# One kernel for attention and two expert layers: head pairs on 64-row scores, one issue order from a list scheduler, 36 weight chunks by way of DRAM

## The chip, the cores and the metric

The kernel runs on 1 core of a Trainium2 chip. The metric is device time in microseconds (us), the median of several executions. Engines that run beside each other: TensorE (PE; the load of its stationary operand is listed as PEld), VectorE (DVE), ScalarE (ACT), GpSimd (POOL), and SyncE (SP), which here only issues DMAs.

## The reference

Everything is float32 at the interface; the weights arrive as float64 and are turned into float32 on the chip.

- Attention: batch 4, 8 heads, 576 tokens, head size 64. `scores = q k^T / 8`, with `min(c_j - c_i, 0)` added, where c is the running sum of `max(s, 0)` along the sequence; causal mask; softmax; times v. That gives x with 2304 rows (tokens) and 512 columns.
- First expert layer: `h = max(x w1, x w2, x w3)` (512 to 768), then `x2 = h w_out` (768 to 512).
- Second expert layer: `h = x2 w_in` (512 to 2048), `g = P(h) / (Q(h) + 1e-6)`, where P is a cubic and Q a quadratic in |h|, then `out = g w_out2` (2048 to 512).

## The kernel before, in words

A float32 product is run as three passes in a format that keeps 12 significant bits: each operand is split into a rounded part hi and the rest lo, and the product is hi hi + hi lo + lo hi (`mm3`, L66). Splitting costs a cast on ACT and a subtraction on DVE or POOL. The value product and the transposes of the attention are plain float32.

**Attention, one head after the other (32 heads).** `load_qk` brings k and q of four heads in one DMA each; `prep_qk` (L177) turns them round with DVE transposes in 32x32 blocks and splits them. The result lies as 32 rows per head with two halves of the head size side by side, so `stage` (L197) copies each head's operands by five more DMAs, from SBUF to SBUF, into tiles `A1`, `B1` and `AB2` with up to 128 rows: the first score matmul contracts 128 rows (hi and lo against hi), the second 68 rows (hi against lo, and four rows that carry the bias). Query rows come in five tiles (64 rows and four times 128), the score blocks in four PSUM banks (`SB`): six blocks, so 12 score matmuls per head (`sc_bank`, L219; the lines L226 and L227). For each block DVE adds the mask and takes the row minimum (L234), ACT takes the exponential with its row sum (L238); `norm` forms the reciprocal on DVE (L244, L245) and POOL scales (L250). `t_bank` transposes the probabilities P on PE (L269, 15 matmuls a head) and copies them out into `PT` (L254 on DVE, L256 on ACT). `pv_pair` (L282) multiplies by v for two heads, each head in its own half of the array's columns (L293), and splits x.

**First expert layer beside it.** `moe1_group` (names m and hs) is 12 matmuls of 288 columns; 144 such groups, 36 for each batch of 8 heads. DVE and ACT take the maximum out of PSUM (L349, L351). A batch's groups can start when the x of its four head pairs is there; they are put between the attention's steps at 4.5 groups a head (`rate`, `credit`, `fill`).

**Weights.** Chunks of 128 x 512 float64 values (512 KB) are loaded and decoded: three bit operations on DVE (L315 to L317), the cast on ACT (L318), the subtraction on POOL (L319). 18 chunks of the first layer (w13) and 18 of the second (`spill`) go through during the attention; the 18 are written to DRAM as hi and lo (512 KB) and read back later. The other 20 (`direct`) are loaded and decoded after the attention's last step, beside the last batch's groups.

**Second half.** For six blocks of 384 tokens: `moe1_out` (mo), then 16 steps of `m2_in` (hp), the rational function on ACT, POOL and DVE (`m2_mid`), and `m2_out` (acc) four steps behind.

**What sets the order.** Tiles are taken from pools; a scheduler of the framework orders the instructions of each engine by a simulated timeline when the program is built. Each engine then runs its queue in order, and waits on semaphores.

Of the kernel before, what the change touches and what calls it, by code (L numbers as in the profile page):

```python
# [14 lines left out]
DRAM = bass.MemoryType.DRAM  # L15


@with_exitstack
def kernel(
# [34 lines left out]
    # query row tiles (first row, rows); columns seen by a tile end at its last row  # L54
# [3 lines left out]
    # the first heads take turns on three sets of score operands, the others on two  # L58
    NF = H

    dma = nc.sync
# [13 lines left out]
    ps_mm = ctx.enter_context(tc.tile_pool(name="ps_mm", bufs=2, space=PSUM))  # L75
# [10 lines left out]
    # weights of the layer at work, 18 chunks of 512 columns in two parts  # L86
# [3 lines left out]
    ps_at = open_pool("ps_at", space=PSUM)  # L90
# [3 lines left out]

    h_dram = dram.tile([DF1, NT], F32, name="h_dram")
    ext_dram = dram.tile([N, 4, 2, S], F32, name="ext_dram")

# [4 lines left out]
    A1 = [at.tile([128, S], F32R, name=f"A1_{i}") for i in range(2)]  # L102
    B1 = [at.tile([128, S], F32R, name=f"B1_{i}") for i in range(2)]
    AB2 = [at.tile([68, 2, S], F32R, name=f"AB2_{i}") for i in range(2)]
    P = [[at.tile([n, 128 * (i + 1)], F32, name=f"P{y}_{i}") for i, (_, n) in enumerate(IT)] for y in range(2)]
    # transposed probabilities of a head pair: row i of column block j at SKEW j + i
# [3 lines left out]
    smalls = [at.tile([128, 4, NI], F32, name=f"small{i}") for i in range(3)]  # L110
    for t in smalls:
        nc.gpsimd.memset(t, 1.0)

    sc = p1.tile([N, 2, S], F32, tag="x", bufs=8, name="sc")
    hl = {}

    def load_qk(g, eng=dma):
        """four heads' k and q rows, 18 tokens a partition, into the place of the hi parts"""
        for nm, src, c in (("k", k, 2), ("q", q, 3)):
            t = at.tile([128, c, 2, S], F32, tag=f"hl{nm}", name=f"hl_{nm}{g}")  # L120
            eng.dma_start(
                out=t[:, 0].rearrange("p c t -> p (c t)"),
                in_=src[g // 2, 4 * (g % 2):4 * (g % 2) + 4].rearrange("h (p f) d -> (h p) (f d)", p=32))
            hl[nm, g] = t

    v_t = {}
    ve_t = {}

    def load_v(pr):
        """v rows of a head pair, the last 64 tokens of two pairs at once"""  # L130
        b, h = divmod(2 * pr, H)
        for n in (2 * pr, 2 * pr + 1):
            v_t[n] = at.tile([128, 4, D], F32, tag="v", bufs=4, name=f"v{n}")
            dma.dma_start(out=v_t[n], in_=v[b, n % H, 0:512].rearrange("(j p) d -> p j d", p=128))
        if pr % 2 == 0:
            ve_t[pr // 2] = at.tile([64, 4, D], F32, tag="ve", bufs=2, name=f"ve{pr // 2}")
            dma.dma_start(out=ve_t[pr // 2], in_=v[b, h:h + 4, 512:576].rearrange("h p d -> p h d"))

    dma.dma_start(out=sc[:, 0, :], in_=s.rearrange("b h s -> (b h) s"))
    load_qk(0)  # L140

    ext = [p1.tile([N, 2, S], F32, tag="x", bufs=8, name=f"ext{r}") for r in range(4)]
    third = [p1.tile([128, 2, S], F32R, tag="x", bufs=8, name=f"third{r}") for r in range(2)]
    A1.append(third[0][:, 0])
    B1.append(third[0][:, 1])
    AB2.append(third[1][0:68])

    def ab_of(n):
        return n % 3 if n < NF else n % 2

    for r in range(4):
        nc.gpsimd.memset(ext[r][:, 1 - r // 2, :], 1.0)
    make_identity(nc, ident)
    nc.gpsimd.memset(mask, 0.0)
    nc.gpsimd.affine_select(
        out=mask[:, S - 128:S], in_=mask[:, S - 128:S], compare_op=ALU.is_ge,
        fill=-BIG / scale, base=0, pattern=[[-1, 128]], channel_multiplier=1)
    for y in range(2):
        for i, t in enumerate(P[y]):
            nc.gpsimd.memset(t[:, 128 * (i + 1) - 64:128 * (i + 1)], 0.0)  # L160
# [3 lines left out]
    c = sc[:, 1, :]  # L164
    nc.vector.tensor_scalar(sc[:, 0, :], sc[:, 0, :], 0.0, 1.0 / scale, ALU.max, ALU.mult)
# [249 lines left out]
    for n in range(3):  # L415
        stage(n)
# [232 lines left out]
```

## Time and profile before

| | us |
|---|---|
| median of 3 runs | 989.79 (988.73 to 990.48) |
| span of the profiled execution, first to last instruction | 991.3 |
| PE busy | 923.2 (93%) |
| DVE busy | 694.2 (70%) |
| ACT busy | 507.9 (51%) |
| POOL busy | 407.5 (41%) |

The profiled execution is one run more; its span is 1.5 us above the median. Busy time of PE is a union of matmuls that overlap in the pipeline, so matmul costs are better read from one start to the next. [...] "Idle before" of a group is the time for which its engine stood still ahead of it.

### The profile page before, as it was taken

Reading aid. Unit: us, or ns where it says so; the run is one execution under the profiler, and the core shown is the slowest. Engines: PE = TensorE matmul, PEld = TensorE weight load, DVE = VectorE, ACT = ScalarE, POOL = GpSimd, SP = SyncE. Lnnn points to the kernel's source line nnn. Section 1 sums busy time; section 2 is a strip of 40 time slices with the busy share of each in tenths; the row PEclk is TensorE's granted clock in tenths of the full one; section 3 lists DMA queues with packets and bytes.
Section 4 is the critical chain, followed back from the end, with each engine's and each line's share of the span. In section 5 each row is a group of like instructions: output and inputs, shape, how many; then the busy total and the mean of one; then the engine's idle time right before and its main releaser. Section 6 shows DMA issues by size and latency. Waiting matters only on the chain.

```text
span 991.3 us, 16031 instructions
## 1 busy us (share of the span) xinstructions
PE 923.2 (93%) x5488; PEld 827.2 (83%) x5488; DVE 694.2 (70%) x1580; ACT 507.9 (51%) x1137; POOL 407.5 (41%) x463
## 2 busy tenths in 40 slices
PE   1688998999989899999979999999999999999997
PEld 1556797888788788999979999999999999999996
DVE  4657787666566574429966886984985885886786
ACT  3656555544444354413235655654664663764664
POOL 2445554435443352203434533542442452452453
PEclk9897999899999899999989999999999999999999
DMA  8886687677787876018883002002000100200000
GB/s 193 195 211 124 178 209 187 162 225 180 211 248 209 230 183 153 20 53 268 277 274 129 1 1 80 1 1 80 1 1 31 50 1 1 80 1 1 33 1 32
DMA packets 77569, 111.87 MB, mean 113 GB/s; under 512 B 24976, under 2 KB 53136, under 8 KB 77488
## 3 DMA queue, kind: packets, MB, share of 16 engines
q1 hardware_dynamic: 77488, 110.86, 40.3%
q8 instruction: 43, 0.70, 0.3%
q14 instruction: 38, 0.31, 0.1%
HBM read 60.70 MB, written 21.82 MB: 83 GB/s over the span
## 4 chain that ended last, share of the span: by engine, by line
PE 65%; DMA 13%; DVE 11%; issue 4%; ACT 3%; POOL 3%; SPq 1%; POOLq 0%; DVEq 0%; ACTq 0%
PE hp L71 18%; PE acc L584 17%; PE m L71 12%; PE mo L71 7%; PE pv L293 5%; PE tr L269 4%; DMA AB<-hl_k 2%; DVE P L234 2%; PE sc L226 1%; PE sc L227 1%; DMA raw<-in_moe_w_in_dram 1%; POOL q L553 1%; POOL q L554 1%; DMA hl_k<-in_k_dram 1%; DVE hs L351 1%
## 5 line engine op out<-in xcount | busy, mean ns | idle before, releaser
L71 PE MATMUL m<-x,w 128*128 128x288 f32 x1728 | 260.1, 305 | 14.5 <-DVE hs L351 14.4
L71 PEld LDWEIGHTS m<-x,w 128*128 128x128 f32 x1728 | 240.8, 194 | 24.8 <-DVE hs L351 19.2
L584 PE MATMUL acc<-ws,g 128*128 128x512 f32 x864 | 217.6, 394 | 1.5 <-ACT g L570 1.5
L553 POOL TENSOR_SCALAR q<-a,cf 128x384 f32<-128x384 f32 x96 | 92.7, 965 | 264.4 <-ACT a L551 249.3
L71 PE MATMUL hp<-x,w2i 128*128 128x384 f32 x1008 | 189.8, 337 | 0.0
L584 PEld LDWEIGHTS acc<-ws,g 128*128 128x128 f32 x864 | 160.9, 188 | 31.0 <-ACT g L570 2.3
L71 PEld LDWEIGHTS hp<-x,w2i 128*128 128x128 f32 x1008 | 177.2, 188 | 7.1 <-ACT x L535 0.9
L250 POOL TENSOR_SCALAR P<-P,small 128x192 f32<-128x192 f32 (+4 forms) x160 | 88.3, 570 | 100.4 <-DVE small L244 39.1
L238 ACT ACTIVATE P<-P,small 128x576 f32<-128x576 f32 (+4 forms) x160 | 88.6, 555 | 61.7 <-DVE small L234 61.4
L554 POOL TENSOR_TENSOR q<-q,a 128x384 f32<-128x384 f32 x96 | 104.6, 1090 | 8.0
L555 DVE TENSOR_TENSOR t<-hp,t 128x384 f32<-128x384 f32 x96 | 52.9, 551 | 58.0 <-ACT t L552 57.9
L565 ACT ACTIVATE a<-q,cf 128x384 f32<-128x384 f32 x96 | 59.3, 617 | 64.6 <-POOL q L554 64.4
L269 PE MATMUL tr<-ident,P 128*128 128x128 f32 (+2 forms) x480 | 78.0, 287 | 11.7 <-DVE small L234 11.1
L71 PE MATMUL mo<-h,w2o 128*128 128x384 f32 x432 | 82.3, 343 | 5.3 <-DVE hs L351 5.3
L567 DVE SCALAR_TENSOR_TENSOR q<-q,cf,a 128x384 f32<-128x384 f32 x96 | 72.5, 755 | 18.1 <-ACT a L566 17.7
L71 PEld LDWEIGHTS mo<-h,w2o 128*128 128x128 f32 x432 | 77.6, 193 | 7.0 <-DVE hs L351 5.6
L570 ACT CAST g<-t 128x384 fp32r<-128x384 f32 x96 | 49.2, 513 | 65.3 <-DVE t L569 65.3
L269 PEld LDWEIGHTS tr<-ident,P 128*128 128x128 f32 (+2 forms) x480 | 56.6, 143 | 27.1 <-DVE small L234 11.0
L293 PE MATMUL pv<-PT,v 128*64 128x320 f32 (+3 forms) x384 | 69.8, 423 | 8.2 <-issue 6.8
L234 DVE CUSTOM_DVE_ANT_0 P<-sc,mask 128x320 f32<-128x320 f32 (+4 forms) x160 | 62.5, 420 | 18.1 <-PE sc L227 18.0
L226 PE MATMUL sc<-A,B 128*128 128x288 f32 (+2 forms) x180 | 55.4, 333 | 19.4 <-DMA B<-hl_q 16.9
L351 DVE TENSOR_TENSOR hs<-m,hs 128x288 f32<-128x288 f32 x96 | 43.1, 449 | 36.6 <-PE m L71 27.1
(257 smaller groups left out, 1273.4 us busy)
## 6 DMA issues: line engine op xcount, KB each, us to landing
ws<-w_dram SPq DMA_DIRECT2D x18, 512.0 KB, 6.6
A<-hl_k SPq DMA_DIRECT2D x30, 288.0 KB, 4.0
B<-hl_q SPq DMA_DIRECT2D x30, 288.0 KB, 5.5
raw<-in_moe_w_in_dram SPq DMA_DIRECT2D x14, 512.0 KB, 5.7
h_dram<-hs SPq DMA_DIRECT2D x48, 144.0 KB, 3.6
h<-h_dram SPq DMA_DIRECT2D x36, 192.0 KB, 4.2
hl_k<-in_k_dram SPq DMA_DIRECT2D x8, 576.0 KB, 4.0
hl_q<-in_q_dram SPq DMA_DIRECT2D x8, 576.0 KB, 6.7
```

Source lines behind the costliest of these rows:

```text
L71: nc.tensor.matmul(ps, l, r, start=(i == 0), stop=(i == len(seq) - 1))
L226: nc.tensor.matmul(o, B1[ab][:, r0:r0 + nr], A1[ab][:, j0:j1], start=True, stop=False)
L234: nc.vector.tensor_tensor_reduce(Pn[i][:, j0:j1], ps[0:nr, c:c + j1 - j0], mask[0:nr, m0:m0 + j1 - j0], -scale, sm[0:nr, 3, 0:1] if (i == ...
L238: nc.scalar.activation(out=Pn[i][:, 0:W], in_=Pn[i][:, 0:W], func=ACTF.Exp, bias=sm[0:nr, 0, m:m + 1], scale=-1.0, accum_out=sm[0:nr, 1, m ...
L250: nc.gpsimd.tensor_scalar(t, t, sm[0:nr, 2, SMC[i]:SMC[i] + 1], 0.0, ALU.mult, ALU.add)
L269: nc.tensor.transpose(ps[0:w, o:o + nr], Pn[i][:, 128 * j:128 * j + w], ident[0:nr, 0:nr])
L293: nc.tensor.matmul(ps[64 * y:64 * y + 64, i0 - b0:], lhs, PT[y][0:128 if j < 4 else 64, SKEW * j + i0:SKEW * j + b1], start=(j == 0), stop ...
L553: nc.gpsimd.tensor_scalar(qq, a, cf[:, 5:6], cf[:, 4:5], ALU.mult, ALU.add)
L554: nc.gpsimd.tensor_tensor(qq, qq, a, ALU.mult)
L565: nc.scalar.activation(out=a, in_=qq, func=ACTF.Ln, bias=cf[:, 6:7], scale=1.0)
L567: nc.vector.scalar_tensor_tensor(qq, qq, cf[:, 6:7], a, ALU.add, ALU.mult)
L584: nc.tensor.matmul(acc[n, tt], g[:, ga, ts], w[:, wb, :], start=(fc == 0 and x == 0), stop=(fc == KF2 - 1 and x == 2))
```

## The change

- **Operands.** For each head pair, k and q are loaded so that each head has 64 rows of its own (`load_qk`: a head's second half of columns is loaded 32 elements further on, into the next 32 partitions). One DVE transpose per operand (`prep`) then gives the 64 x 576 operand of both heads in place; it is split into `QK`. The five staging DMAs of a head are gone; two small ones per pair bring the bias rows into `EXT`.
- **Scores.** `scores` runs, for each block, four products (hi hi, hi lo, lo hi, bias) of 64 rows, alternating between the two heads, whose rows lie in partitions 0 to 63 and 64 to 127 and whose results go to two PSUM banks. `norm` takes the two heads' sums together.
- **Weights.** All 38 chunks of the second layer but two (`DIRECT`) are decoded during the attention and written to DRAM as float32 (256 KB), not as hi and lo; they are split after being read back (`load_spilled`, `split`).
- **Order.** Steps are not issued as the source runs: `Plan.add` records each with an engine, a cost in us, a rank and what it reads and writes; `Plan.issue` then goes through them, at each point taking the step that can start first, and by rank among those of one engine that can start at once. PSUM banks are handed out by the plan from one pool of 8. The framework keeps the order of issue (`manual_schedule`).

```diff
-    spill = [("o2", kk) for kk in range(KF2)] + [("i", fc) for fc in range(KF2 - 2, KF2)]
-    direct = [("o", kk) for kk in range(KF1)] + [("i", fc) for fc in range(KF2 - 2)]
-    w2_dram = dram.tile([len(spill), 128, 2, 512], F32, name="w2_dram")
+    DIRECT = [("i", 1), ("i", 3)]
+    spill = [x[1:] for x in need if x[1:] not in DIRECT]
+    w2_dram = dram.tile([len(spill), 128, 512], F32, name="w2_dram")
...
+    LAG = 0.15
+    AHEAD = 5.0
...
+            for e, cand in ready.items():
+                t = engine[e]
+                mine = None
+                for n in cand:
+                    s = steps[n]
+                    start = max(t, est[n], wire - self.AHEAD if s[7] else 0.0)
...
+                    key = (max(start, t + 0.1), s[2], n)
...
+            engine[e] = start + cost
+            if kb:
+                wire = max(wire, start + cost) + kb / 190.0
+                end[n] = wire + 2.0
...
+    ctx.enter_context(tc.manual_schedule())
+    plan = Plan([psum.tile([128, 512], F32, name=f"bank{i}") for i in range(8)])
...
+    def c_mm(n):
+        return 0.013 + n / 2400.0
...
+                for u in range(2):
+                    dm(pr - 1.3, 143, raw[nm][64 * y + 32 * u:64 * y + 32 * u + 32, 0:1120],
+                       x[:, 32 * u:32 * u + 1120], (), [("raw", nm, y, u)])
...
+            ve(pr - 0.6, 0, lambda src=src, T=T: nc.vector.transpose(
+                out=T.rearrange("p (x f) -> p f x", f=18),
+                in_=src.rearrange("p (f d) -> p f d", d=D)[:, :, 0:32]),
...
+            if pr < KM:
+                ve(pr - 0.55, 0, lambda T=T, hl=hl: nc.vector.tensor_copy(hl[:, 0, :], T),
...
+            else:
+                ac(pr - 0.55, S, lambda T=T, hl=hl: nc.scalar.copy(out=hl[:, 0, :], in_=T),
...
+        for y in range(2):
+            ext_dma[pr] = dm(pr - 0.6, 18, EXT[pr % 2].bitcast(F32)[64 * y:64 * y + 4], ext_dram[2 * pr + y],
...
+        ops = [(Q[:, 0], K[:, 0]), (Q[:, 0], K[:, 1]), (Q[:, 1], K[:, 0]), (E[:, 1], E[:, 0])]
...
+            for i, j0, j1, at0 in SB[g]:
+                r0, nr = IT[i]
+                for x, (l, r) in enumerate(ops):
+                    for y in range(2):
+                        h = slice(64 * y, 64 * y + 64)
+                        nc.tensor.matmul(hold[y].bank[0:nr, at0:at0 + j1 - j0], l[h, r0:r0 + nr], r[h, j0:j1],
+                                         start=(x == 0), stop=(x == len(ops) - 1))
...
+        pe(pr + 0.1 * g, sum(4 * max(c_mm(j1 - j0), 0.11) for _, j0, j1, _ in SB[g]), mms,
...
+    S0, S1 = 7.0, 15.0
...
+    def m_rank(b, x):
+        return 4 * b + 4.9 + 4.0 * x / NG
...
+        for i, (kind, x) in enumerate(spill):
+            rank = S0 + (S1 - S0) * i / len(spill)
+            r = raww[i % 2]
+            load_raw(rank - 0.3, r, w2_src(kind, x), ("raww", i % 2))
+            decode(rank, lambda r=r: r, lambda i=i: wx[i % 2], ("raww", i % 2), ("wx", i % 2))
+            dm(rank, 256, w2_dram[i], wx[i % 2].bitcast(F32), [("wx", i % 2)], [("spill", i)])
...
+        dm(rank - 0.4, 256, lambda: w2[sp].bitcast(F32)[:, 1, :], w2_dram[i], [("spill", i)], [key])
+        split(rank, lambda: w2[sp].bitcast(F32)[:, 1, :], lambda: w2[sp], key, key)
```

## Rows read from the trace of the kernel before

**Rows 1.** Windows: busy us (instructions) of PE, PEld, DVE, ACT, POOL; clock, DMA share, GB/s
```profile
0.00:100.00 100.00, 63.16 (x332) 46.65 (x332) 62.62 (x208) 53.88 (x137) 43.82 (x79) 0.86 0.76 181
100.00:500.00 400.00, 380.01 (x2705) 340.31 (x2704) 260.71 (x728) 176.10 (x444) 161.05 (x189) 0.97 0.68 189
500.00:530.00 30.00, 24.73 (x132) 24.41 (x131) 15.05 (x27) 9.00 (x20) 7.19 (x6) 0.89 0.78 272
530.00:991.30 461.30, 455.31 (x2326) 415.81 (x2324) 355.83 (x620) 268.90 (x538) 195.43 (x191) 1.00 0.07 22
```

**Rows 2.** PE's waits, whole span: us in total, times, longest
```profile
PE sc L226 <- DMA B<-hl_q: 16.9, 1, 16.9
PE m L71 <- DVE hs L351: 14.4, 11, 3.6
```

**Rows 3.** Timeline of all engines at the start: start us, duration
```profile
9.48 0.54 SPq L173 DMA_DIRECT2D ext_dram<-ext  x1
...
17.09 2.06 SPq L210 DMA_DIRECT2D AB<-ext_dram  x1
...
21.31 0.58 PE L227 MATMUL sc<-AB 68*128 68x288 f32 x1 [2.99 <-DMA AB<-ext_dram]
```

**Rows 4.** Windows on DVE of L185, L234, L244, L245, L254, L297, in this order
```profile
0.00:530.00 530.00, 36.99 (x32) 0.95 0.70 192
...
0.00:530.00 530.00, 76.17 (x384) 0.95 0.70 192
...
0.00:530.00 530.00, 17.38 (x64) 0.95 0.70 192
...
0.00:530.00 530.00, 10.55 (x64) 0.95 0.70 192
...
0.00:530.00 530.00, 23.89 (x96) 0.95 0.70 192
...
0.00:530.00 530.00, 14.48 (x32) 0.95 0.70 192
```

**Rows 5.** Windows on DVE of the decode lines L315, L316, L317, in this order
```profile
30.00:430.00 400.00, 19.54 (x36) 0.94 0.69 179
...
30.00:430.00 400.00, 27.11 (x36) 0.94 0.69 179
...
30.00:430.00 400.00, 34.18 (x36) 0.94 0.69 179
```

**Rows 6.** Timeline: value product in column halves, then transposes
```profile
126.45 2.81 PE L293 MATMUL pv<-PT,v 128*64 128x256 f32 x20
129.19 0.33 PE L293 MATMUL pv<-PT,ve 64*64 64x64 f32 x4
129.45 0.66 PE L269 MATMUL tr<-ident,P 128*128 128x128 f32 x4
```

**Rows 7.** Timeline: a head's first score matmuls up to the next group; two weight loads
```profile
134.44 0.38 PE L226 MATMUL sc<-A,B 128*128 128x288 f32 x1
...
134.99 1.78 PE L71 MATMUL m<-x,w 128*128 128x288 f32 x12
...
136.61 0.19 PEld L227 LDWEIGHTS sc<-AB 68*128 68x128 f32 x1
136.75 0.14 PEld L226 LDWEIGHTS sc<-A,B 128*64 128x64 f32 x1
```

**Rows 8.** Timeline of PE: first group m, attention's end, second half's start
```profile
100.19 1.05 PE L71 MATMUL m<-x,w 128*128 128x288 f32 x6
...
433.88 18.29 PE L71 MATMUL m<-x,w 128*128 128x288 f32 x136
...
509.42 5.55 PE L71 MATMUL mo<-h,w2o 128*128 128x384 f32 x18 [5.27 <-DVE hs L351]
```

**Rows 9.** DVE's group of L351: count, busy us, mean ns, idle before
```profile
L351 DVE TENSOR_TENSOR hs<-m,hs 128x288 f32<-128x288 f32 x96 | 43.1, 449 | 36.6 <-PE m L71 27.1 <-issue 7.0 <-ACT hs L349 2.0
```

**Rows 10.** Timeline of DVE: one decode step held up
```profile
78.82 4.19 DVE L317 SCALAR_TENSOR_TENSOR w13(0, 2)x<-w13(0, 2)r,w13(0, 2)x 128x512 uint32<-128x512 uint32 x1
```

More of the change, by code (lines that the diff above doesn't have):

```diff
@@ L468 @@
-    w_store()
-    assert nj[0] == len(jobs) and not raws and not stores
-    close_pool("ps_at")
-    close_pool("at")
-    wr = open_pool("wr", side="right")
-    ps_t = open_pool("ps_t", space=PSUM)
-    w2 = {}
-    rb = [p1.tile([128, 512, 2], U32, tag="x", bufs=8, name=f"raw{x}") for x in range(3)]
-    xb = new_raw("xb").rearrange("p f t -> p (f t)").rearrange("p (a f) -> p a f", a=2)
-    xb = [new_wx("xc"), xb[:, 0], xb[:, 1]]
+            col = b * S + hf * HALF
+            dm(rank, 144, h_dram[128 * fc:128 * fc + 128, col:col + HALF], t, [("hs", n)], [("h", b, fc, hf)])
@@ new lines, in coefs @@
+    def coefs():
+        nc.scalar.activation(out=cf[:, 4:6], in_=cf[:, 8:10], func=ACTF.Abs)
+    late = set()
+    for pr in range(NP):
+        if pr:
+            load_qk(pr)
+        prep(pr)
+        load_v(pr)
+        for g in range(4):
+            scores(pr, g)
+            if g == 1:
+                norm(pr, (4, 1, 0))
+        norm(pr, (3, 2))
+        for g in range(4):
+            for y in range(2):
+                flip(pr, y, g)
+        values(pr)
+        if pr == 0:
+            weights()
+        if pr == 0:
+            dm(0.9, 2, cf[:, 0:4], coef_a.rearrange("(o n) -> o n", o=1).to_broadcast([128, 4]), (), ["cf"])
+            dm(0.9, 2, cf[:, 8:10], coef_b.rearrange("(o n) -> o n", o=1).to_broadcast([128, 2]), (), ["cf8"])
+            ac(1.5, 2, coefs, ["cf8"], ["cf4"])
+            ve(1.5, 2, lambda: nc.vector.memset(cf[:, 6:7], 1.0 + 1e-6), (), ["cf6"])
+        if pr % KM == KM - 1:
+            n0 = len(plan.steps)
+            for x in range(NG):
+                experts(pr // KM, x)
+            late.update(range(n0, len(plan.steps)))
@@ new lines, with to_wr, new @@
+    pools = {}
+    def to_wr():
+        close_pool("at")
+        pools["wr"] = open_pool("wr", side="right")
+    plan.add("ctl", 0.0, NP, to_wr, (), ["wr"], pre=[n for n in range(len(plan.steps)) if n not in late])
+    w2 = {}
+    w2_key = {}
+    rb = {}
+    xb = raww[0].rearrange("p f t -> p (f t)")[:, 0:512]
+    xb = [(wx[0], ("wx", 0)), (wx[1], ("wx", 1)), (xb, ("raww", 0))]
+    for i in range(3):
+        def new(i=i):
+            rb[i] = p1.tile([128, 512, 2], U32, tag="x", bufs=8, name=f"rb{i}")
+        plan.add("ctl", 0.0, NP, new, ["wr"], [xkey(NP + i), "x order"])
@@ new lines, with to_p2 @@
+    pre = range(len(plan.steps))
+    n_d = n_s = 0
+    for i, (_, kind, x) in enumerate(need[:20 + 2 * KF1]):
+        rank = NP + 0.5 + 4.5 * i / 32
+        if (kind, x) in DIRECT:
+            load_direct(n_d, rank)
+            n_d += 1
+        else:
+            load_spilled(n_s, rank)
+            n_s += 1
+    t2 = {}
+    def to_p2():
+        close_pool("p1")
+        p2 = pools["p2"] = open_pool("p2", side="left")
+        for kk in range(KM):
+            t2["x", kk] = p2.tile([128, 2, TB], F32R, name=f"x2_{kk}")
+        for nm, bufs in (("t", 4), ("a", 2), ("q", 2)):
+            for i in range(bufs):
+                t2[nm, i] = p2.tile([128, TB], F32, name=f"{nm}2_{i}")
+        for i in range(4):
+            t2["g", i] = p2.tile([128, 2, TB], F32R, name=f"g2_{i}")
@@ new lines, in m2_out, with new @@
+            pe(rank, 3 * 0.231, mms, [kg, w2_key["o2", fc]], [("acc", n, tt)], take=[hold] if fc == 0 else ())
+            if fc == KF2 - 1:
+                key, = hkeys(1)
+                o = {}
+                def new(o=o, tt=tt):
+                    o[0] = pools["p2"].tile([128, DM], F32, tag="h", bufs=KF1, name=f"o{n}_{tt}")
+                plan.add("ctl", 0.0, rank, new, ["p2"], [key, "h order"])
+                on_v = n == NBLK - 1 and tt == 1
+                (ve if on_v else ac)(rank, DM, lambda o=o, hold=hold, on_v=on_v: (
+                    nc.vector.tensor_copy(o[0], hold.bank) if on_v else nc.scalar.copy(out=o[0], in_=hold.bank)),
+                    [("acc", n, tt)], [key], free=[hold])
+                r0 = n * TB + 128 * tt
+                dm(rank, 256, out[r0:r0 + 128, :], lambda o=o: o[0], [key], [("out", n, tt)])
```

799 lines of the change are left out of this document (430 added, 369 removed).

## The prediction

> **What bounds the kernel now.** I read the windows first, as the span falls into stretches with different limits [rows 1]. The reader should see PE busy for 455.3 of the last 461.3 us at full clock: the second half is bound by PE and has nothing to give. The first 530 us hold all the rest. Up to 100 us PE is busy for 63.2 us at a clock of 0.86; from 100 to 500 it is busy for 380.0 of 400 us at 0.97; from 500 to 530 for 24.7 of 30 us at 0.89. DVE is busy for 260.7 of the 400 us, so it has room; ACT (176.1) and POOL (161.1) have more. Then the list of PE's waits: one of 16.9 us on a staging DMA at the start, and 14.4 us in eleven waits on the DVE step that takes a group out of PSUM [rows 2]. Last, PE's timeline for three marks: the first group m at 100.19 us, the attention's end at 433.88, where only groups are left, and the second half's first product at 509.42, after a stall of 5.27 us on DVE [rows 8]. So PE is the bound from 100 us on, and ahead of that the chain of DMA, DVE, ACT and POOL for the first eight heads is.
>
> **The change part by part.**
>
> *First batch.* Gone are five DMAs a head, between them some 870 KB. The second part of the first score product started only at 21.31 us, when the bias rows had come, whose DMA was issued at 17.09 behind the other staging on SP's queue [rows 3]. After the change the last bias row still goes to DRAM at about 9.5 to 10 us [rows 3], and the way back stands behind eight loads of k and q only. With some 3 us for each way (the bias rows took 21.31 - 17.09 = 4.2 us from issue to use in a full queue) scores start at 15.5 us (13 to 19). From there I take DVE as the limit for four pairs. Work per pair [rows 4]: transposes 36.99 / 16 = 2.31; mask and minimum 76.17 / 16 = 4.76; reciprocals, halved as two heads share them, (17.38 + 10.55) / 32 = 0.87; copies into PT 23.89 / 16 = 1.49; splits of x 14.48 / 16 = 0.91. New on DVE for the first pairs are two casts, for which I take 0.4 each (a copy as wide as half of one is 0.25 in the same rows, the transpose as wide 1.16). Sum 11.1 us, four times 44.5, and 1.5 for the first pair's lo parts. A weight chunk's decode is (19.54 + 27.11 + 34.18) / 36 = 2.24 us [rows 5]; about eight of the first layer's 18 fit in or are needed by then, 18 us. So the first group m starts near 15.5 + 44.5 + 1.5 + 18 = 80 us: 20 us earlier. Bounds: 73 with five chunks, 95 where the probabilities, one buffer per head, make each pair wait for the pair before (5 us gained).
>
> *Scores.* Before, 12 matmuls a head. In [rows 7] the first four of a head, 960 of its 3200 columns, take 134.99 - 134.44 = 0.55 us, so a head takes 1.83 and a pair 3.67. After, a pair has 48 matmuls of 64 rows, the same columns each, in 24 rounds of two. Side by side, a pair again costs 3.67; one after the other, 7.33. No row shows two halves of the array's rows at work at once. The nearest shows its column halves: 24 value matmuls of one pair take 129.45 - 126.45 = 3.0 us [rows 6]. [...] Two weight loads a round might still bind: a load of 128 columns takes 0.05 us more than one of 64 [rows 7], which gives 0.10 for 128 and 0.2 for two, so 20 rounds at 0.2 and four at 0.1, 4.4 us a pair, 0.7 more than now. Only the 12 pairs beside which PE is full count: from -12 (rounds of 0.11 us, as the value product's 28 in 3.0) through 0 and +8.4 to +44 (3.67 x 12). I take +8, the load bound.
>
> [...] The row on mode changes: the transposes begin at 129.45 while the last value matmuls run to 129.52 [rows 6], so leaving column halves costs PE no visible time. [...]
>
> *Order.* From 100 to 500 us PE stands for 20.0 us, and the missing 0.03 of clock is another 12 us of full speed [rows 1]. The plan works from costs, puts groups wherever the attention can't start, and no longer has staging DMAs (288 KB four times and more a head) between steps. I credit two thirds: -13 and -8 (bounds 0 and all 32). The late groups cover it: at the attention's end 75 us of PE were still to run [rows 8].
>
> *Weights.* 18 more decodes move from the tail into the attention, 18 x 2.24 = 40 us of DVE. From 80 us to the attention's end near 410, DVE would hold 12 pairs at 10.3 (the casts now on ACT), 10 and 36 decodes, and 72 of the 96 maxima at 0.449 [rows 9]: 124 + 103 + 32 = 259 of 330 us. Cover is there, so 0. Traffic falls: the staging was 32 x 864 KB = 27.6 MB, the doubled loads of k and q add 8.9 MB, and 36 stores and reloads of 256 KB are as much as 18 of 512. In the tail the stall of 5.27 us and the clock of 0.89 (3.3 us of 30) should go, as DVE has no 20 decodes there: -7 (0 to -8.6). The 18 more splits after reading back fall to ACT and POOL, idle for most of the tail.
>
> *Second half.* Same products in the same sequence, PE full: 0 (-2 to +10, if a reloaded chunk comes late).
>
> Sum on the span of the profiled run: 991.3 - 20 + 8 - 13 - 8 - 7 = 951.3. That span is 1.5 above the median of 989.8, so 949.8: I say 950.
>
> **The rivals.**
>
> *Rows one after the other* (0.16). The two heads' matmuls don't overlap: +44 in place of +8, so 986; the first pairs hide theirs. For it: 68 rows cost nearly as much as 128 now, so fewer rows alone save nothing. Against it: the column halves [rows 6]. With part of the loads overlapping it ends nearer 970.
>
> *The waits stay* (0.16). The order is fixed from costs, the chip's differ, and PE waits as often as now: 950 + 13 + 8 = 971. For it: PE now waits for DVE steps whose time varies [rows 2, 10]. Against: the long first-layer groups are free to move.
>
> *Drain at each change of mode* (0.06). A pair enters and leaves 64-row mode for four banks, eight changes; bounded by 0 [rows 6] and by one whole short matmul of 0.33, 2.6 a pair, 32 over 12 pairs: up to 982. [...]
>
> *DVE becomes the bound and the kernel is slower* (0.12). DVE's steps between SBUF tiles are at times held up: one decode step took 4.19 us [rows 10], where L317's mean is 34.18 / 36 = 0.95. If each of the 46 decodes after 80 us is held up so once, that is 46 x 3.2 = 149 us on the 259; the attention would end at 80 + 408 = 488, and 36 groups of 1.6 us (as 18.29 us for 136 of their matmuls [rows 8]) follow, so the second half starts at 546 and the time is near 1026. It decides from where DVE's work passes 372 us (attention's end at 452, second half at 509 as now): three quarters of the decodes held up. At nine tenths: 1010. Against it: the mean of 2.24 already holds such delays.
>
> *The order isn't as planned* (0.04): if the framework's order remains, only the operands change, within 0.2% of 990 (what a measurement of this kernel can tell from no change).
>
> **How the numbers follow.** Forecast 0.46, its own range 925 to 965; the others as given. Best bounds together: 991.3 - 27 - 12 - 32 - 8.6 - 1.5 = 910, not likely all at once; I set the low end at 918, the high end at 992, past the rows' rival, and leave the DVE case out. Faster by over 0.2%: 0.46 + 0.15 + 0.15 + 0.06 = 0.82; same 0.05; slower 0.13, the DVE case and a little of the others.
>
> **What would show it.** First group m at 73 to 95 us; score pairs whose two matmuls start within some 10 ns (right) or one length apart (wrong); a pair's scores in 3.7 to 4.4 us of PE; no wait on DVE ahead of the first mo, which starts near 470; PE's idle time between under 10 us; DVE under 85% in the attention. Wrong altogether: PE waiting for DVE in the attention by tens of us, or a second half longer than 480 us from the first mo.

## The result and the profile after

The changed kernel takes **952.31 us** (median of 4 runs, 952.23 to 953.43) against 989.26 for the kernel before (4 runs, 987.43 to 990.48): a ratio of 0.9625, 95% interval 0.9596 to 0.9653. The forecast was 950, range 918 to 992. The profiled execution has a span of 950.1 us; before it was 991.3.

The page of the kernel after: busy time and share of each engine, the granted clock of TensorE in 40 slices (in tenths of its full speed), the bytes.

```profile
PE 904.2 (95%) x5872; PEld 806.4 (85%) x5872; DVE 740.8 (78%) x1522; ACT 501.5 (53%) x1137; POOL 395.8 (42%) x466
...
PEclk9998999999999999999999999999999999999999
...
DMA packets 72259, 92.52 MB, mean 97 GB/s; under 512 B 25296, under 2 KB 53456, under 8 KB 72176
```

PE's marks in the timeline of the kernel after, to be read against [rows 3, 8]: the first score product, the issue of the bias rows' way back, their product, the first group m, the attention's end, and the second half's first product. (The columns are start and duration; the helper that records all matmuls of this kind is L174, and PSUM tiles are now all named bank.)

```profile
11.01 1.40 PE L379 MATMUL bank<-kT,qT 64*128 64x288 f32 x6 [11.01 <-DVE qT L341]
...
15.68 1.78 SPq L216 DMA_DIRECT2D EXT<-ext_dram  x4
...
19.72 0.86 PE L379 MATMUL bank<-EXT 64*128 64x288 f32 x2 [7.30 <-DMA EXT<-ext_dram]
...
84.23 0.66 PE L174 MATMUL bank<-x,w 128*128 128x288 f32 x3
...
385.80 14.46 PE L174 MATMUL bank<-x,w 128*128 128x288 f32 x107
...
455.89 15.78 PE L174 MATMUL bank<-h,ws 128*128 128x384 f32 x90
```

These marks cut the span into three stages: A up to the first m, B from there to the first product of the second half, C the rest. Windows of the kernel before, cut at its own marks (100.19 us, and 500.85, where its first product of the second half ran ahead of the stall of [rows 8]); columns as in [rows 1]:

```profile
0.00:100.19 100.19, 63.34 (x332) 46.67 (x332) 62.81 (x210) 53.88 (x137) 44.01 (x79) 0.86 0.76 181
100.19:500.85 400.66, 380.68 (x2709) 341.14 (x2709) 260.82 (x729) 176.72 (x445) 161.31 (x190) 0.97 0.68 189
500.85:991.30 490.45, 479.19 (x2450) 439.37 (x2448) 370.58 (x645) 277.29 (x555) 202.16 (x196) 0.99 0.11 37
```

And of the kernel after:

```profile
0.00:84.23 84.23, 54.53 (x456) 40.64 (x456) 70.35 (x185) 45.38 (x124) 53.30 (x83) 0.98 0.62 159
84.23:455.89 371.66, 366.59 (x2972) 328.86 (x2969) 269.48 (x706) 171.67 (x454) 155.66 (x183) 1.00 0.61 177
455.89:950.10 494.21, 483.08 (x2450) 436.93 (x2448) 401.01 (x632) 284.44 (x560) 186.86 (x201) 1.00 0.09 27
```

The first column after each window is its length; the clock is the share of its full speed that TensorE was granted. Stage A is 16.0 us shorter, B 29.0 shorter and C 3.8 longer: together 41.2 less. In B, PE's idle time fell from 20.0 to 5.1 us and the granted clock rose from 0.97 to 1.00. In C the count of matmuls is the same; the stall of 5.27 us is gone and yet the stage is longer.

PE's busy time in B fell too, by 14.1 us, and the value products account for about as much. Windows of B on their lines, L293 before and L477 after (length, PE busy, clock, DMA share, GB/s):

```profile
100.19:500.85 400.66, 53.81 (x355) 0.97 0.68 189
84.23:455.89 371.66, 37.10 (x336) 1.00 0.61 177
```

That is 0.152 us a matmul before and 0.110 after, some 14 us at the same count. In the order before, one head's matmuls often ran without the other head's beside them: four of a pair stood alone, 1.11 us from 109.54 to the next matmul's start at 110.65, ahead of the 24 of [rows 6]. In the kernel after all 28 of a pair follow one another, 3.0 us to the next start at 129.37.

```profile
109.54 1.19 PE L293 MATMUL pv<-PT,v 128*64 128x256 f32 x4
...
126.36 2.81 PE L477 MATMUL bank<-PT,v 128*64 128x256 f32 x24
```

### The profile page after: what moved, and what is told of

Its sections match the earlier page's. It is cut to its first block, busy times and chain, and to the rows that moved or that the text cites. A ratio compares the mean times of both kernels' runs of the same rounds, so it can differ in the third digit from the quotient of the medians.

```text
span 950.1 us, 16586 instructions
## 1 busy us (share of the span) xinstructions
PE 904.2 (95%) x5872; PEld 806.4 (85%) x5872; DVE 740.8 (78%) x1522; ACT 501.5 (53%) x1137; POOL 395.8 (42%) x466
## 3 DMA queue, kind: packets, MB, share of 16 engines
HBM read 69.61 MB, written 21.82 MB: 96 GB/s over the span
## 4 chain that ended last, share of the span: by engine, by line
PE 47%; DVE 32%; ACT 9%; issue 5%; POOL 3%; DMA 2%; SPq 1%; DVEq 0%; POOLq 0%; ACTq 0%
PE bank L174 31%; DVE a L768 7%; DVE q L766 6%; PE bank L793 6%; DVE t L770 4%; PE bank L379 4%; PE bank L435 4%; PE bank L477 3%; DVE t L755 2%; ACT a L765 2%; DVE t L754 2%; DVE wx L512 2%; POOL P L422 2%; ACT a L746 2%; ACT g L772 2%
## 5 line engine op out<-in xcount | busy, mean ns | idle before, releaser
L174 PE MATMUL bank<-x,w 128*128 128x288 f32 x1728 | 250.2, 300 | 2.9 <-ACT x L484 2.4
L174 PEld LDWEIGHTS bank<-x,w 128*128 128x128 f32 x1728 | 232.7, 189 | 10.0 <-issue 3.6
L793 PE MATMUL bank<-ws,g 128*128 128x512 f32 x864 | 219.8, 398 | 6.2 <-ACT g L772 4.4
L793 PEld LDWEIGHTS bank<-ws,g 128*128 128x128 f32 x864 | 160.2, 189 | 42.0 <-DVE g L773 7.0
L174 PE MATMUL bank<-x,ws 128*128 128x384 f32 x1008 | 191.0, 338 | 1.1 <-ACT x L732 1.0
L174 PEld LDWEIGHTS bank<-x,ws 128*128 128x128 f32 x1008 | 177.8, 188 | 10.0 <-ACT x L732 2.2
L422 POOL TENSOR_SCALAR P<-P,small 128x576 f32<-128x576 f32 (+4 forms) x160 | 93.4, 601 | 110.8 <-ACT P L401 48.9
L401 ACT ACTIVATE P<-P,small 128x192 f32<-128x192 f32 (+4 forms) x160 | 88.5, 556 | 50.1 <-DVE small L394 49.6
L753 POOL TENSOR_TENSOR q<-q,a 128x384 f32<-128x384 f32 x96 | 108.5, 1130 | 8.0
L766 DVE SCALAR_TENSOR_TENSOR q<-q,cf,a 128x384 f32<-128x384 f32 x96 | 74.0, 771 | 30.2 <-ACT a L765 30.1
L768 DVE SCALAR_TENSOR_TENSOR a<-q,a 128x384 f32<-128x384 f32 x96 | 86.6, 902 | 3.1
L435 PE MATMUL bank<-ident,P 128*128 128x128 f32 (+1 forms) x480 | 73.3, 286 | 11.1 <-POOL P L422 10.3
L174 PE MATMUL bank<-h,ws 128*128 128x384 f32 x432 | 76.1, 337 | 0.0
L174 PEld LDWEIGHTS bank<-h,ws 128*128 128x128 f32 x432 | 75.2, 189 | 0.6
```

The lines of the kernel that those rows point to most:

```text
L401: ac(pr + 0.1 * g + 0.04, 0, lambda Pi=Pi, W=W, m=m, nr=nr: nc.scalar.activation(out=Pi[:, 0:W], in_=Pi[:, 0:W], func=ACTF.Exp, bias=sm[0: ...
L422: po(pr + 0.3, 0, lambda t=t, nr=nr, m=m: nc.gpsimd.tensor_scalar(t, t, sm[0:nr, 2, m:m + 1], 0.0, ALU.mult, ALU.add), [("rc", u, c0)], [( ...
L435: nc.tensor.transpose(hold.bank[0:w, o:o + nr], P[y][i][:, 128 * j:128 * j + w], ident[0:nr, 0:nr])
L753: po(rank, 0, lambda: nc.gpsimd.tensor_tensor(t2[kq], t2[kq], t2[ka], ALU.mult), [ka], [kq], cost=1.02)
L766: ve(rank, 0, lambda: nc.vector.scalar_tensor_tensor(t2[qq], t2[qq], cf[:, 6:7], t2[a], ALU.add, ALU.mult), [ka], [kq], cost=0.62)
L768: ve(rank, 0, lambda: nc.vector.scalar_tensor_tensor(t2[a], t2[qq], 2.0, t2[a], ALU.subtract, ALU.mult, reverse0=True), [kq], [ka], cost=0.56)
```

## The experiments

Each is the changed kernel with one edit. Times are medians; a ratio is to the kernel before.

### Scores: are the two heads side by side, and what is it worth?

**Same rows.** Both heads use rows 0 to 63. (The second head's products are then formed from the first head's operands.)

```diff
-                        h = slice(64 * y, 64 * y + 64)
+                        h = slice(0, 64)
```

> The changed kernel with both heads' score products taken from the same 64 rows (partitions 0 to 63, so the second head's scores are computed from the first head's operands); counts and shapes as before. Computing head by head in program order did not take the side by side away: the trace of that run shows the two halves' matmuls within 16 ns of each other all the same. Theory 1, the two halves of the array's rows run side by side whatever the order, and only sharing the rows ends it: eight 288-column matmuls take 8 x 0.134 = 1.07 us instead of 0.54, a pair's scores 3 us more, so 970 to 990. Rival, a 64-row matmul is as quick alone: within 4 us of 952.

Measured 993.09 us (992.29 to 998.95), ratio 1.0066 (1.004 to 1.0093): 40.8 us slower than the change, which is more than all that the change gained. Of it 11.6 us fall in A (first m at 95.82) and 28.7 in B. The scores of one bank here, and then those of another bank in the kernel after, whose first block is the same:

```profile
281.99 1.06 PE L379 MATMUL bank<-kT,qT 64*128 64x288 f32 x6
282.89 0.42 PE L379 MATMUL bank<-EXT 64*128 64x288 f32 x2
283.15 0.81 PE L379 MATMUL bank<-kT,qT 64*128 64x192 f32 x6
```

```profile
260.12 0.67 PE L379 MATMUL bank<-kT,qT 64*128 64x288 f32 x6
260.62 0.29 PE L379 MATMUL bank<-EXT 64*128 64x288 f32 x2
260.76 0.31 PE L379 MATMUL bank<-kT,qT 64*64 64x64 f32 x6
260.90 0.23 PE L379 MATMUL bank<-EXT 64*64 64x64 f32 x2
261.05 1.85 PE L174 MATMUL bank<-x,w 128*128 128x288 f32 x12
```

Eight matmuls of 288 columns take 1.16 us on the same rows (281.99 to 283.15) and 0.64 on two row halves (260.12 to 260.76). The single starts behind the last rows, and those of the weight loads (us):

```
matmuls, head 0 / head 1: 260.119 / 260.122, 260.354 / 260.358, 260.488 / 260.491, 260.624 / 260.627
weight loads:             260.117 / 260.120, 260.224 / 260.229, 260.358 / 260.361, 260.490 / 260.494
```

Two matmuls start 3 to 4 ns apart, and their loads 3 to 5; a round costs 0.134 us, where the forecast's +8 had 0.2. That two loads a round bind, the reason for it, is wrong. What costs instead is the change between products of 128 rows and of 64: the first round of a bank takes 0.235, and from the last score matmul (260.903) to the next group's first (261.054) it is 0.151 where such short rounds come every 0.06. The groups on either side lose as much again: from their last matmul (259.899) to the first score it is 0.22, and from 261.054 to the second matmul behind the scores (261.294) 0.24, where matmuls of a group start every 0.13. That is about 0.2 on entering and 0.2 on leaving, four banks a pair, 1.6 us. What the array does in that time the starts don't show.

**One head after the other in program order.**

```diff
-                for x, (l, r) in enumerate(ops):
-                    for y in range(2):
+                for y in range(2):
+                    for x, (l, r) in enumerate(ops):
```

> One edit to the changed kernel: in each score block the four products of one head run, then the four of the other, so neighbouring matmuls nearly always use the same 64 rows. Same instructions, same count. Theory 1, the alternating halves run side by side: a pair's scores go from 3.9 us of PE (eight matmuls of 288 columns take 0.64 us in the changed kernel's trace) towards 7.3 us, eight such matmuls take about 1.0 us or more, and with PE full beside 12 pairs the time grows by up to 40 us, to between 975 and 992. Rival, the two halves don't overlap and the rounds were cheap for another reason: eight matmuls still take 0.64 us and the time stays within 3 us of 952.

Measured 955.72 us (954.23 to 956.68), ratio 0.9654 (0.9595 to 0.9713): 3.4 us more, nothing like same rows' 41. In its trace the second head's matmuls still run beside the first's:

```profile
263.11 0.69 PE L379 MATMUL bank<-kT,qT 64*128 64x288 f32 x6
263.61 0.32 PE L379 MATMUL bank<-EXT 64*128 64x288 f32 x2
```

Eight matmuls of 288 columns again take 0.63 us, with starts at 263.109 / 263.122, 263.346 / 263.363 and so on, though the program has all of one head's ahead of the other's: the bias product (EXT) of the first head, fourth in the program, starts behind six of the `kT,qT` products, three of which are the second head's. So in this trace matmuls on one half of the rows start ahead of one on the other half that comes earlier in the program: that each engine runs its queue in order does not hold for PE here.

### The order: what makes it good?

**The framework's own order.** The operands, the weights' way and the plan's PSUM banks stay; the instructions are put in order by the framework.

```diff
-    ctx.enter_context(tc.manual_schedule())
```

> One line removed from the changed kernel: the framework's own scheduler orders the instructions again, starting from the plan's issue order, on the same operands, buffers and weights' way. Theory 1, the order is what took PE's waits away between the first group m and the first product of the second half: the waits come back, about 15 us of idle time and some 10 us of clock, and the time is 970 to 980. Rival, the operands did it (no staging DMAs to wait for), and any reasonable order does as well: within 5 us of 952.

Measured 1035.25 us (1034.23 to 1035.88), ratio 1.0462 (1.0409 to 1.0515): worse than before. Its windows, cut at its own marks, and the one of B on the value products' line:

```profile
0.00:122.72 122.72, 80.24 (x403) 60.49 (x403) 99.71 (x228) 51.17 (x134) 68.60 (x91) 0.70 0.64 167
122.72:548.47 425.75, 405.89 (x3022) 356.47 (x3023) 245.19 (x663) 166.77 (x445) 135.84 (x174) 0.96 0.46 138
548.47:1032.40 483.93, 476.90 (x2450) 437.81 (x2448) 379.66 (x632) 278.33 (x560) 209.30 (x201) 1.00 0.09 27
...
122.72:548.47 425.75, 51.02 (x364) 0.96 0.46 138
```

A is 38.5 us longer than in the kernel after. In B PE idles for 19.9 us at a clock of 0.96, where the kernel after idles for 5.1 at 1.00, and a value matmul costs 0.140 us. As the banks were assigned for another order, part of this may be the banks'. C alone is shorter, by 10.3 us; the section on the second half comes back to it.

**No costs.** Every step costs next to nothing in the plan; only the ranks and dependencies order it.

```diff
+        cost = min(cost, 0.001)
         self.steps.append((eng, cost, rank, fn, pre, tuple(take), tuple(free), kb))
```

> The changed kernel with every step's cost set to 0.001 us in the plan, so that its clock moves by the fixed lag of 0.15 us a dependency and by DMA transfers alone, and ties go by rank: the plan no longer knows that an engine is busy. Theory 1, ranks and dependencies carry the order and the lag is enough: within 6 us of 952. Rival, the plan must at least know that an engine's work takes time, or it puts steps in the queues in an order in which they can't start: 975 or more, with PE waiting for DVE and ACT between 100 and 450 us.

Measured 1203.06 us (1199.3 to 1203.68), ratio 1.2177 (1.2128 to 1.2226). PE's longest sums of waits (us in total, times, longest):

```profile
PE bank L436 <- POOL P L423: 39.9, 30, 3.5
PE bank L175 <- ACT w L520: 37.1, 14, 5.7
```

Without durations the plan issues matmuls as soon as their inputs have been issued, and PE stands in front of each.

**One cost for each engine.**

```diff
+        cost = cost if eng in ("ctl", "sp") else {"pe": 1.1, "dve": 0.65, "act": 0.56, "pool": 0.87}[eng]
```

> The changed kernel, with the plan's costs made blind: every step of an engine has one cost (PE 1.1, DVE 0.65, ACT 0.56, POOL 0.87 us), so the order no longer follows measured times. Theory 1, the order's worth comes from costs close to the chip's: waits return and the time is 965 or more. Rival, dependencies and ranks carry the order, costs matter little: within 5 us of 952.

Measured 954.4 us (951.92 to 956.98), ratio 0.9646 (0.9594 to 0.9698): the same within the runs' spread. So durations are needed, but a mean for each engine did as well here.

### The first batch and the bytes

**Bias rows ahead of the second pair's loads.**

```diff
-                       x[:, 32 * u:32 * u + 1120], (), [("raw", nm, y, u)])
+                       x[:, 32 * u:32 * u + 1120], (), [("raw", nm, y, u)], pre=[ext_dma[0]] if pr == 1 else ())
```

> The changed kernel with the second pair's eight loads of k and q held until the first pair's bias rows have landed. In the changed kernel PE waits 7.3 us for those rows, whose DMA is issued at 15.68 us behind the second pair's loads. Theory 1, the start is late by SP's queue alone: the bias rows come some 3 us earlier, and as DVE is the limit until 84 us the whole moves by 2 to 4 us, to 948 to 950. Rival, the second pair's transposes get as much later, and nothing is gained: 951 to 954.

Measured 951.06 us (950.72 to 952.08), ratio 0.9637 (0.9607 to 0.9666). The bias product starts at 16.32 us instead of 19.72, yet the first m at 89.08 instead of 84.23, with 472 matmuls ahead of it instead of 456, and the time is 1.3 us less: most of the 3.4 us doesn't reach the end. The second pair's loads were held back for it, so the run doesn't give the delay's price by itself.

**Junk copies.** Twelve DRAM to DRAM copies of 144 KB a pair, which depend on nothing.

```diff
+                for u in range(3):
+                    dm(pr - 1.3, 0.001, junk[pr, 6 * (nm == "q") + 3 * y + u], x, (), [("junk", pr, nm, y, u)])
```

> The changed kernel with twelve more DMAs a pair of 144 KB each from k and q in DRAM to a DRAM tile that nothing reads (1.73 MB a pair, as much as the staging moved before), on SP's queue. Theory 1, what the staging cost before was the waiting for it, not the traffic: within 5 us of 952. Rival, traffic and SP's issue time did: later loads of k, q and weights, PE waiting for DVE transposes and group weights, 965 or more.

Measured 1065.79 us (1065.4 to 1066.25), ratio 1.0797 (1.0764 to 1.083). It doesn't answer its question: free and independent in the plan, the 192 copies went out at the start, the bias product came at 57.17 us and the first m at 197.4. From there to the second half it takes 371.68 us, as the kernel after's 371.66. It shows that a delay of the first batch passes whole into the end: A is 113.2 us longer, the time 113.5.

**Spread copies.** Each loaded quarter tile of k and q is also written to DRAM twice, known to the plan.

```diff
+                    for e in range(2):
+                        dm(pr - 1.2, 143, junk[pr, 8 * (nm == "q") + 4 * y + 2 * u + e],
+                           raw[nm][64 * y + 32 * u:64 * y + 32 * u + 32, 0:1120], [("raw", nm, y, u)], ())
```

> Adds 18.3 MB of traffic spread over the attention: each quarter of the raw k and q tiles (143 KB) is, once loaded, also written twice to a DRAM tensor that nobody reads; the plan knows of these copies. That is about the 19.4 MB by which the change lowered the total (111.87 to 92.52 MB). Theory: the staged traffic that went was worth little by itself, as DMA stood at 0.62 of its time: 951 to 958, all of it in the first batch. Rival: the traffic that the change removed is a good part of what the order seemed to give (the clock of stage B and 15 us of idle): 970 to 985, with matmuls waiting for DMA between the first m and the end of attention.

Measured 1022.04 us (1020.39 to 1029.94), ratio 1.0348 (1.0308 to 1.0388), but with 36.7 MB more, twice what was meant (256 copies). So once more with `range(1)`:

> The run before it added 36.7 MB, not the 18.3 MB it was meant to (its trace: 256 copies of 140 KB, 129.25 MB in all), and so more than the kernel before ever moved. Here each quarter tile is written once: 18.4 MB more than the change, 111 MB in all, as much as the kernel before (111.87 MB), under the change's order and plan. Theory: what the change gained it gained by its order and its scores side by side, and the traffic that went with the staging was worth little by itself, as DMA has room at 0.61 of its time; the 70 us of the double copies came from a DMA share of 0.81 and up: 952 to 962. Rival: traffic counts by the byte, 70 us for 36.7 MB, so half of it costs half: 980 to 990, and the whole gain of the change could be put down to its 19.4 MB less.

Measured 980.5 us (978.98 to 981.94), ratio 0.9895 (0.9866 to 0.9925), with 110.88 MB in all: in the rival's range, though by the byte half of 70 us would have been 35 and not 28. Its windows, cut at its own marks:

```profile
0.00:100.53 100.53, 63.97 (x472) 47.52 (x472) 77.05 (x208) 48.48 (x137) 54.73 (x82) 0.85 0.71 204
100.53:484.63 384.10, 371.93 (x2955) 330.65 (x2953) 263.92 (x683) 167.81 (x442) 159.04 (x183) 0.99 0.69 201
484.63:980.10 495.47, 483.19 (x2450) 436.71 (x2448) 401.32 (x632) 284.63 (x560) 186.69 (x201) 0.99 0.09 27
```

Against the kernel after, A is 16.3 us longer (as long as before the change, at a clock of 0.85) and B 12.4. The bias product starts at 20.05 us, 0.3 later than without the copies; it is the chain behind it that is slower. In A and B, PE's waits for the normalized probabilities grow:

```profile
PE bank L439 <- POOL P L426: 25.5, 27, 4.8
```

In the kernel after they are `10.3, 12, 2.9`. What stays open: a copy is bytes, a place in the one queue that issues all DMA, and a cost in the plan, which then came out with another order. The run doesn't separate the three. Nor are the copies what the change removed: the staging went from SBUF to SBUF, while they write to DRAM. The pages count 21.82 MB written to HBM, the chip's DRAM, before and after the change, and 40.17 MB here.

### The weights' way

**Twenty chunks straight from the input.** Instead of 2, 20 of the second half's chunks are loaded and decoded in the tail, as in the kernel before; their first steps are also kept ahead of the second half's tiles.

```diff
-DIRECT = [("i", 1), ("i", 3)]
+DIRECT = [("o", kk) for kk in range(KF1)] + [("i", fc) for fc in range(KF2 - 2)]
```

> The changed kernel with the weights split as before: 20 chunks (all six of w_out, the first 14 of w_in) loaded and decoded beside the last batch's groups, 18 by way of DRAM. Theory 1, the way through DRAM is worth the stall ahead of the second half: DVE is behind with 20 decodes there, the first mo waits 5 us or more, and the time is 957 to 965. Rival, with DVE relieved of 18 decodes (40 us) in the attention the time is the same or less, 945 to 953, as DVE and not the tail's stall is what counts.

Measured 968.38 us (966.81 to 970.39), ratio 0.9788 (0.9737 to 0.984): 16.1 us more. First m (83.8 us) and the attention's end (384.6) stay. The tail's waits are back, now ahead of the second expert layer's first products, which read the split x2:

```profile
PE bank L174 <- ACT x L734: 14.3, 6, 9.8
...
PE bank L174 <- DVE x L735: 3.3, 1, 3.3
```

They are 17.6 us of waiting. The forecast's -7 for the tail had only the old stall and its clock in it; now that the attention ends 48 us earlier, the same decodes in the tail would hold PE for longer than they did.

### The second half: why longer?

Around 530 us the kernel after takes 4.75 us from one chunk's matmuls to the next one's, where most chunks of the stage take 4.17. The timeline of one such chunk on DVE, then on POOL and ACT:

```profile
529.30 0.65 DVE L766 SCALAR_TENSOR_TENSOR q<-q,cf,a 128x384 f32<-128x384 f32 x1 [0.57 <-ACT a L765]
529.99 1.25 DVE L768 SCALAR_TENSOR_TENSOR a<-q,a 128x384 f32<-128x384 f32 x1
531.28 0.62 DVE L770 SCALAR_TENSOR_TENSOR t<-t,cf,a 128x384 f32<-128x384 f32 x1
531.82 0.55 DVE L754 TENSOR_TENSOR t<-bank,t 128x384 f32<-128x384 f32 x1
532.40 0.61 DVE L755 SCALAR_TENSOR_TENSOR t<-t,cf,bank 128x384 f32<-128x384 f32 x1
...
534.05 0.66 DVE L766 SCALAR_TENSOR_TENSOR q<-q,cf,a 128x384 f32<-128x384 f32 x1 [0.57 <-ACT a L765]
...
529.64 1.19 POOL L753 TENSOR_TENSOR q<-q,a 128x384 f32<-128x384 f32 x1
...
533.05 0.49 ACT L746 ACTIVATE a<-bank 128x384 f32<-128x384 f32 x1 [0.60 <-DVE t L755]
533.44 0.52 ACT L765 ACTIVATE a<-a 128x384 f32<-128x384 f32 x1
```

It is a locked cycle: DVE's L766 waits for ACT's L765, which stands in ACT's order behind L746 of the next chunk, which waits for DVE's L755. Two things lengthen it: the wait of 0.57, and L768, which takes 1.25 us beside POOL's L753. Its mean over the second half is 902 ns, where before the same step took 580.

**The low parts of h on GpSimd**, for token blocks 1 to 5, to test whether VectorE's load is the limit.

```diff
-        ve(rank, TB, lambda: nc.vector.tensor_tensor(
+        (po if n else ve)(rank, TB, lambda: (nc.gpsimd if n else nc.vector).tensor_tensor(
             h_hl[n, kk][:, 1, :], h_hl[n, kk]...
```

> In the second half the low parts of h of token blocks 1 to 5 are formed on GpSimd instead of VectorE; all else is the change. Theory: the second half is about 12 us slower than a steady 79.6 us a block would make it because VectorE is its limit whenever it also forms h's low parts (4.07 us a chunk plus 0.55). Then the block's pace goes from 80.1 back to about 79.6, the waits of the chunk's output matmuls go, and the time to 945 (941 to 950), faster than the change by 3 to 10 us. Rival A: GpSimd's three long operations a chunk (0.70 + 1.13 + now 0.9 or more) slow VectorE's instructions beside them further, as VectorE's 902 ns against 580 ns before suggests: 952 to 965. Rival B: TensorE sets the pace and the waits are only the hand-over's slack: 951 to 953.

Measured 957.88 us (955.93 to 958.09), ratio 0.9679 (0.9655 to 0.9704): 5.6 us slower, so the theory fell, and rival A's 952 to 965 holds it. The split takes 1129 ns on GpSimd where it took 555, and L768's mean rises to 934. And the kernel after has no such split at all between 516 and 541 us, where the cycle is locked: it can't have been the cause of the lock.

**Costs as the trace shows them**, for five operations of a second-half chunk (the edit in short: line and cost).

```diff
-  (L751) cost=0.97   (L753) cost=1.02   (L766) cost=0.62   (L768) cost=0.56   (L770) cost=0.62
+  (L751) cost=0.70   (L753) cost=1.13   (L766) cost=0.77   (L768) cost=0.90   (L770) cost=0.68
```

> Only the plan's costs of five operations of the second half are set to the durations that the trace after shows (GpSimd 0.70 and 1.13 us instead of 0.97 and 1.02; VectorE 0.77, 0.90 and 0.68 instead of 0.62, 0.56 and 0.62). Theory: the order of the second half is planned with a VectorE 0.55 us a chunk too short, so that its instructions are issued in an order that the real ones can't keep; with the true ones the first block's late chunks lose less: 946 (942 to 950). Rival: as with one cost for each engine, the exactness of costs gives nothing and VectorE's load is what it is: 950 to 955.

Measured **945.47 us** (944.35 to 948.07), ratio 0.9563 (0.954 to 0.9587): 6.8 us below the change and so faster than both kernels; its runs and the change's don't overlap. The window of its last stage:

```profile
455.01:942.30 487.29, 479.21 (x2450) 436.72 (x2448) 412.04 (x632) 282.90 (x560) 202.51 (x201) 1.00 0.09 27
```

Its timeline in the stretch that was locked, on DVE and then POOL:

```profile
528.86 1.05 DVE L766 SCALAR_TENSOR_TENSOR q<-q,cf,a 128x384 f32<-128x384 f32 x1
529.95 0.56 DVE L768 SCALAR_TENSOR_TENSOR a<-q,a 128x384 f32<-128x384 f32 x1
530.54 0.62 DVE L770 SCALAR_TENSOR_TENSOR t<-t,cf,a 128x384 f32<-128x384 f32 x1
531.08 0.61 DVE L766 SCALAR_TENSOR_TENSOR q<-q,cf,a 128x384 f32<-128x384 f32 x1
...
528.48 1.02 POOL L753 TENSOR_TENSOR q<-q,a 128x384 f32<-128x384 f32 x1
```

Here DVE is busy for longer (412.04 us against 401.01) and the stage is 6.9 us shorter, so DVE's load was not the limit; the order of its steps was. Two chunks are interleaved, and none of these steps of DVE waits for ACT. Of the 6.9 us, 4.95 fall in the first block of 384 tokens, the one with the locked chunks: from its first product to the next block's it is 80.61 us (455.01 to 535.62) where it was 85.56 (455.89 to 541.45). The hold-up has not gone: here it falls on L766 (1.05 us), which now runs beside L753. The framework's own order, above, says the same more strongly: it runs this stage's 2450 matmuls in 483.93 us, 10.3 less than the plan's order, with DVE busy for 379.66. One order was tried with these costs; that true costs always find the better one is not shown, since one cost for each engine did no harm.

## Why the prediction was right, and where it was not

The time fits (950 against 952.31), but partly because errors cancel. By stages of the span, in us:

| | forecast | measured |
|---|---|---|
| A, first batch | -20 | -16.0 |
| B, scores +8, idle -13, clock -8 | -13 | -29.0 |
| C, tail -7, second half 0 | -7 | +3.8 |
| sum | -40 | -41.2 |

*First batch: right in its reason, 4 us too large.* Scores in full went on at 19.72 us and not 15.5: the way back of the bias rows was issued at 15.68, behind sixteen loads of k and q rather than eight, the second pair's too. Taking the delay away was worth 1.3 us at the end (bias first). DVE was busy for 70.35 of 84.23 us, near the limit that the sum assumed; its eight casts took 6.8 us where the sum had 3.2, one of them 3.19 (at 28.07). That the first batch waited for DMA before, the chain of work that ended last supports: between the bias product and the first m it holds these among others in the kernel before, and no DMA at all in the kernel after.

```profile
27.01 5.33 DMA AB<-hl_k
32.41 3.95 DMA hl_k<-in_k_dram
...
59.34 6.45 DMA AB<-hl_k
```

With the single copies A is back at 100.53, within the limits said there. And the removed DMAs don't do it alone: without the plan's order A is 122.72.

*Scores: the side that decides was right, the reason for +8 wrong.* The +8 takes it that two halves of the rows work side by side. No row of the kernel before showed that, and for halves of the columns the 24 matmuls in 3.0 us [rows 6] don't show it by themselves: there it is seen in the starts of the kernel before (two products of 64 rows at 129.190 and 129.197) and in the 0.28 us a matmul of its four that stood alone, where a pair's 28 in one piece take 0.11 each in the kernel after. Row halves do run side by side in the kernel after (two starts 3 to 4 ns apart; eight matmuls of 288 columns in 0.64 us, and in 1.16 on the same rows), and same rows give 993 where the rival said 986; but the rival put all of it beside the last 12 pairs and said that the first pairs hide theirs, and 11.6 us fell in A, so its nearness is partly luck. The load bound isn't there (0.134 us a round); about 0.4 us a bank for the change between 128 and 64 rows is. From each bank's first score to the next operation the four banks of a pair take 1.16 + 0.93 + 1.01 + 0.79 = 3.89 us; with some 0.2 a bank that the neighbouring groups lose it is 4.7, about 1.0 above the forecast's 3.67 for before. Over 12 pairs that is some 12 us, an estimate: +8 was near in size by luck. I took such a change at nothing from [rows 6], from ends that are modelled; by the starts it is not nothing: 0.149 us in the kernel before too, from the last value matmul (129.303) to the first transpose (129.452), where two rounds of these value matmuls start 0.107 apart.

*Order: under-credited, and one term of it not seen.* I took two thirds of 20.0 us of idle and 12 of clock. The idle time fell by 14.9 (I said 13) and the clock's loss went altogether (I said 8 of 12): the granted clock of B was 1.00. The value products I priced at nothing, as I had read a pair's cost from 24 matmuls in a row [rows 6] and not seen the four ahead of them; in one piece they cost some 14 us less in B. Idle time, clock and value products, less the scores' 12, come to about the 29.0 us, roughly, as part of the value products' 14 is the clock's. These are sums from two traces; no run took the value products apart by themselves, but they cost more again under the framework's order. By the order's runs the gain isn't that of any order: with the framework's order the same operands are 46 us slower than before the change, without durations 214.

*Traffic: not priced at all in stage B.* The prediction told of the bytes and gave them no term there. The single copies add 12.4 us to B. Taking away the order or the scores side by side, or adding the copies, costs 83, 41 or 28 us, of a gain of 37: the three don't add. That the copies' price is that of bytes is not shown.

*Tail: the stall went, as said.* There is no wait ahead of the first product. Its cover, DRAM in place of decoding, is worth 16 and not 7, as the twenty direct chunks show.

*Second half: the step that failed.* "Same products in the same sequence, PE full: 0." Without the stall of 5.27 us and the missing clock up to 530 us (3.3 us) the stage before would take 490.45 - 8.6 = 481.9 us; it takes 494.2, +12.3 and past the bound of +10. The sequence of PE was the same; that of DVE, ACT and POOL wasn't, and in a stage with DVE at 81% the order within a chunk can lock PE at 4.75 us. New costs give back 6.9 of the 12.3, and the framework's order 10.3 (483.93 us): nearly all of the 12.3 is the order of the engines beside PE. How much of it each wait holds is open. The prediction named "a second half longer than 480 us from the first mo" as a sign of being wrong altogether: it is longer, but that sign was badly set, as the kernel before took 490.45, and 481.9 without its stall and slow clock.

*The rivals.* Rows one after the other: refuted by the starts 3 to 4 ns apart. Waits stay: refuted, 5.1 us of idle time in B. Drain: that the array drains is not shown; that the changes cost time is, and 0.4 us a bank is more than half of the bound of 0.66. DVE as the bound of the attention: DVE is busy for 269.48 of 371.66 us, 73%. Order not as planned: refuted, and the framework's order would not have been neutral.

## What to carry to other kernels

A sequence that is the same on the engine that bounds a stage says nothing of the others: where a second engine is nearly as busy (here DVE, 81%), look at the order within one turn of the loop on every engine, since waits from engine to engine can close into a cycle longer than any engine's work (here 4.75 us a chunk, where most took 4.17). Value products of two heads took 0.110 us a matmul where the order kept them together, and 0.152 where parts of them stood alone: look for pieces that run alone. When several parts of a change are each needed, take them away one at a time and don't add the losses. The plan by costs needed durations (1203.06 us without); true ones for operations that hold each other up are cheap to try (945.47 us).

## What was unexpected of the hardware

Matmuls on one half of the rows started ahead of an earlier one in program order on the other half (one head after the other: starts 13 and 17 ns apart, and 0.63 us for eight). A change from 128 rows to 64 and back cost about 0.4 us, half of it in the groups beside (kernel after, 259.899 to 261.294).

Operations of DVE took longer beside one of POOL: L768 0.56 us alone (new costs, at 529.95) and 1.25 beside L753 (kernel after, at 529.99), and in the other order it was L766 that took longer beside L753 (1.05 us at 528.86, against 0.61 at 531.08). Why they take longer is not shown.
